# Another recorded program order for a decay-attention and feed-forward kernel, with four weight loads behind the first product

## The chip, the cores and the metric

The kernel runs on one core of one Trainium2 chip. The metric is device time in microseconds for one execution, from the start to the end of the program. The engines are named as in the profile: PE is TensorE's matmuls and PEld its weight loads, DVE is VectorE, ACT is ScalarE, POOL is GpSimd, and SP is SyncE, which here mainly issues DMAs. Each engine runs its own instructions in program order; an instruction waits by semaphores for what the others must have done first.

## The reference, cut to what matters

Four sequences (B = 4) of 768 steps go through a linear attention with eight heads of width 48 whose state decays with a complex factor. The 384 outputs of each step then go through a feed-forward layer with a rational activation.

```python
# attention: per batch b and head h, over the 768 steps t
mag = sqrt(a_re**2 + a_im**2); scale = minimum(mag, 0.999) / (mag + 1e-6)
S = (a_re + 1j * a_im) * scale * S + outer(k[t], v[t])   # the product enters the real part
y[t] = q[t] @ S.real
# feed-forward: x is y as 3072 x 384, w_in 384 x 2048, w_out 2048 x 384
h = x @ w_in
P = a0 + a1*h + a2*h**2 + a3*h**3
Q = 1 + abs(b0) * abs(h) + abs(b1) * h**2
out = (P / (Q + 1e-6)) @ w_out
```

## The kernel before, in words

**Units and pairs.** The sequence is cut into six chunks of 128 steps. A chunk of one batch is a unit; there are 24 units, in 12 pairs. Units u0 and u1 (chunk 0, batches 0 and 1) are the first pair, u2 and u3 the second. A unit goes through these functions:

- `norm`: loads the decay factors (AA), forms squares, magnitudes (three short scans, line 524, into MM) and the tangent of each step's angle (T).
- `angle` and `table`, for two units at once: sum up the angles by a scan, take off whole turns into CO and T, and take sines and cosines on ACT. A small copy (line 547, `thc`) keeps the last angle for the next chunk.
- `outer`: loads the queries and keys (QK, 384 KB) and the values (V, 320 KB); scales by the decay (`e`, line 585; line 586; `rho`, line 588; the QK product, line 589); forms two Q products (line 591), one with the cosines and one with the sines; and copies these by six DMAs of 128 KB (line 596, issued on line 345) from SBUF to SBUF into HQ, the layout that TensorE reads. There are two HQ tiles.
- `attn`: on TensorE the transposes of the keys (line 611), the scores (line 624), the values (line 642) and the states (line 662). VectorE multiplies the scores by a mask (ST, "mask product"). VectorE or ACT takes the transposes out of PSUM (kT).

**Feed-forward.** `ffn` runs once per pass. A pass has first products (line 701: x times w_in into one of three ph banks), an elementwise chain on ACT, VectorE and GpSimd, and reduce products (line 717: g times w_out). The first two passes are called with `whole`: they use fp32 weights, six instructions in a product. Later passes use split weights (wiH and wiL, wh and woL), nine in a product. The elementwise instructions are recorded by helpers, so that they have the lines of these: 351 for VectorE and GpSimd, 366 and 357 for ACT.

**Weights.** `fold` brings in w_in as 12 blocks wi (512 wide, 512 KB) and w_out as 16 blocks wo (384 wide, 384 KB). The DMA is issued on line 345; a block then takes a step on ACT (lines 431 or 439, or an equivalent on GpSimd) and two steps on VectorE (lines 447 and 449). The staging tiles are wh0 to wh2 and the four g tiles, so a load waits until a staging tile is free. `halve` later splits the weights for the passes after the second.

**Fillers.** `rouse` records matmuls without a use (line 673, into the bank po1; each shows as a pair of instructions). An order may put each on PE, or on SP, where it is no instruction at all.

**The order.** The program is first collected as a list of 2597 operations, each with its inputs (`preds`) and the engines that can run it (`ways`). The string `ORDER`, written out in the file, then fixes the place and the engine of each:

```python
code = array.array("H", zlib.decompress(base64.b85decode(ORDER)))
for step in code:
    x = (x + step) % 65536
    o = self.ops[x % 4096]
    o.eng = list(o.ways)[x // 4096]
    if not o.preds <= done:
        return None
    order.append(o)
```

The operations are emitted in this order, so it is the program order of each engine and of each DMA queue. Where an operation stands ahead of one of its inputs, `recorded` returns None and `list_schedule` searches an order by its own costs.

Of the kernel before, what the change touches and what calls it, by code (L numbers as in the profile page):

```python
# [232 lines left out]


ORDER = (
    "c-lQ!2Y8m%6@I@zJ0!U`EE#PQz)_{e5vUZEB?z(vg$gR5EKvhNnIXsq6Gen1j0izMhKwo%P-#I?P*jMvMW_`*0%5cW`EJ4pS^w#KZ>Z1z{Nww+JI;B}d){;I"
# [3 lines left out]
    "|1w8M;T41+PZqQcIsLuV!=pIXqOdSAFt2tSt=}o}E;bF&q~(c14*{&;oKQw=e#@T=o3#uU<<|Z;acprzER_oSlvjM1Yut;Gk`h=^8->OAPCmtd;+mGtm5GU-"  # L240
    "DfOGtipxa0yeJyYJYl3x2JiIBgC6Zj!WfB2$}OIYS>oxFeuZp8X)qh(xu?b`yyt8Q(B6USc5-1JVo@olgE8=QG_8#&s|rSYU8RH0Gy%t-8j)Z<FI9z`w>fgM"
    "WFu30NgHpXq$tnS!!Wca4?aMIUhR*^yAq)z%nlV^7R8xiXe}p@Dxr+|e)%J#aYXv*Q1dDlsS-bnc4WyZ`3L#7m|l2zk?+!kgfk_<t+Z#HsUZ?oGG3-jQ!hh;"
    "GKHvxVXX3yYrap|T|65F!TY>wGA)L-1)Oi8?sKTL)HCSc2%_Mb7Uc9+T$d4K_bPtdk;D0<Aimq_`h3<2tz<b8b(ERT$a<KM3Yj4b5P^C`E)z32V-fFlz%cSM"
    "8Y|UFW=npsyXWDHglXn+V^^Gy6>6A?!GmP`&IGUc5Sn3~{??DgWNEHT`~><R&bNor9GxO-ouzMz;hnS6M~-1T21$u%Wb*#K`k#J|6v-PzDc5>|B0nfu%=T##"
    "jcf9j%lT?73tpym4RxOQwBj3NFxv6Dl4EM*Wx4LRK(Q>=P4HhoONyCwHR>6EGpbaC8IIK|O)W1@l~f&yMgBy6k113sX1N+?w#oza{+}{R#vw)r<u#L~ZZi=$"
    "ubP<tI4!p$;4-fo8|69v-bOB5mPY!V^kkm?&eV!krAS64pBnHyHZTiU$qSsb9Ix=nbjiRb&J_8Us7{vua72OXVBWx)xLh+LX;e`%^W-(`<GNea5YrB;B~rKH"
    "Zl{s&hce#NsaS=<+daF>Ec{kd$mzdIJ3g6-rgA5Brajhhr$fk>R2-7eBnErrgiOW9@*v*hh>!8O6iQPZK!2i~%*glDANn=KIGkR8t9qIFl7=N@?+Cm@_1eRy"
    ")G)b%NNKBQ=&y>>AS%~yt-tVzzT7|)nZbCr!sECpE6C^<Y1=2#i&tODzZj({NWmicSUqJ@sTb?zOMEJS=gK=}J|o(LSFO;I<7RP2J&e-(%{cLc0djgQtio;M"
    "vxC@&<IMF3a8*5ImeH#h@U0$N>R}>U>j^}^y!0qF=tmhAH>xb4|Lxlx&PJXZZN8G_9B&b$CdvjX&H-LmOK-Gi1Rf@WB6C!sZ+TfO8?iu*GC?^m_hJhX@$heI"
    "*>)L(9NK)G^M}&k1@b<#;&Iy8kR!TaxLR-iCEL|3vsZqLbJAV^<bR+-%}l&)by^27gFHQ^R+<j7lm6^*`55W;-YIt9r?}1r8Nkm^WFQW6_XhlIPcChcpH!yV"  # L250
    "E{CW9XU!U7G>|&iidlM$kuO#8CIssluYuIMD^&hu-Olu8rnkf!da&P5D^o?($DkJiT70L1-0_AC<6bYxYK&2NCKi|F8zOR@PY!U`^)jA2AC$K-LAo#}j9TwU"
    "vx@vAqwzV%RY*T-)n2Z)R3>npKTAHxUn8<z$i=7BZhG5Ct;NpZ=&}X2!pUV?dzH9f;Z-B%PMOmqYCk&aC;STHkj|X2+4l=}1atJ=)UhqnM*rwvlUQ8DpTt(@"
    "8fk<gx!@G~A@pJ-I-x+?;tMsMtZ0KDXiW(#$|rIj-Q{ko;Blfi*&GaZ^a5Zs^#b2kqN(^<Yy?`;l4V5wudbSQBZB4BkW-BQ@9_vTz7_B6lBRkIt$CU{5<x|J"
    "(?4$`s9xrdsYquA1yD%*{~@)Kj5}DxAH!MI7|M)63&zpIX6Es2!Qp}Bao0_}!`Q=ko$cSGwyzSSV!67)FYbOrBJ`trn5=z(wiU>IP6^{#5kA*@SgltQ1^a42"
    "-|nV$vFJg47{S=S;^*ki%*hZu%@~OD$i5ax3vZ<Ry^4CVoLX=vaZ15mRO7CAN{{z%kl6t;;&Up4Ma0wd%nx#tJQ#uynS<B4=Fd37T6RRNg<p%c^$A+hN&bcp"
    "qyeq##XPOgxua><PppA^IHE5Zvr+ECAN6`h(Z;(6Ge&dNhmxkx`bBb>QFs<M11?E_KHn=Z;i}7wJeL(cIMyepzHkw50L!F4+V}_L8PrE6qaLBpQyGKo>cZ&r"
    "*Yu$)9%4*vUVE&+lbvSwjms_DL|wDh{Q~pIBR|h@&3$U5S;z0;y!wq>fqe!pI_+*u<kq_0$zoR`&#5%do6ox0Nk7Jjg_AWsv4dH%5D&=_b^%Gczo`_fd)=uT"
    "c3uSX<L>lIOij?!>Hhb;u41JtlfCFCRgBOIHHDVsb4~(zJqn+(lW5OuydqWVQ|?w4Y|XstjLq^Sl`w)@*_nA?A$iQt8&rl+^7UC~Ux9kWtR)UZRDmB(RU57T"
    "WQKBHv!rvhwVt`5o~Mp)RfCM}fUiiU(&nb@XWaHMH%Cx~gmt=r7@w7fUOMY@B+*)<hfo)7#=L5ognO+{>RILjy%70Goi^hoTa7o_j9D5MN;UhS39N!k*)OHj"
    "x@Hdjb7Y!Fqy{)kx5`-wi=X7%-eD$p4PZ7$-;@lU%C#5!bLin(Ji#t>F=wU8T;_(=iP!aYKMqs)YaLlK5)I`|u6CW>O#pTL^^ilqBTWuR)k-<lCX?%**CA$+"  # L260
    "yo&^ss48D%9M1{?OjUD;OEznAwb+W4Ma~YUZR}F?296reJFk*S9yPSC$D;r2Emz22nC+(}S4DCD`}%-iDO+52P1SF@8WPU<#xq*I*b^O=&iWv`>#<np#x%!s"
    ">|^gK9zm}s>I_L^^xvZ5RLCmsG@5HIVjmSkmV6|W$p2+T<-EU`$c0dc`s>#0v@Y6}^dkRB-rFL%)a!QamOqw0>`CX|(iYETQ3VyNTsU5WJrURwOGn1G2{F&q"
    ")BM*lUuNPcm2wCBuc=7q9&>R7DZyo4O3>mO$ND=A?Nzq7t8@+#Tg`J%x!C;ejFU1<zTwV4sHrB|<<D3u>RnXn=bfkNI@)w0n}4I*ntbN(0qI7bCDOte#%T|^"
    "C1i3F;(Z%_@36Ib8^-Gx^l^Dp&Q*@FaweNy%$551n`+BWY^w}rR};_=m<pbcnv<CgsT^gDasyg8gxb**OYjWQ{hFTdkh{HB{60mz68$c)T&p`ZRosfk1m<o9"
    "v*2N>iG8wGm75q9&pI2U!%P*q)JXc0jn6vHM6oX#i<Jll+0*G*#$qAsO%`><p5pQ)Gwx{Fc4k;5?ar4ACRN^%8gg-|ZswmtG?mnMr`ApCq)BHMUZOqLruXF>"
    "UQ_QN&G(!_gmEu>j_}wKc{-9jn?iovpqDSR`;7JG%3H3d7OFrPyR>O|MKAQzdB(_QM;7VkO_F5}*Fm(amU}GWx@TmGT4HV|KD5y7ltOiz#6IvmnP$%u6*5fs"
    "Fr%4`v)Mtv=QMi_US^GI%6RtIU-E?bFze%7?mw7z&t!(#U7o>TsAns6k<6wKvw0_%NVN-Y^menG*~Vv4))yi^lo>w2DgFSSNv*CX@SId8IaH!eD&6F;&eu@w"
    "?k6LX`MgMWk=c91&K`vAtd%|Kc^K}uJ(a_&7xTncj#1j`dNy~Orf2)}$nPq0xEnrV*WUvP%n8O<?CI_?7yBlx664qbA0c<<5$E^JD9LkHTC470WHzz_E@U3w"
    "@6LoLIpz*CQr2LX>c_Q?vZMZ<*fyp;hPs_>o|GASp1%=|sjuR&3&#ofohDmgBOjo>H{}O<_MLi=`r8Z_dA7Jgt0G`mjJZ{9w(<OU*;(?ae8yF(*;zeC{tXZ2"
    "dUaY<LDle_{>31Uwr032uL@3fC*2R^X=LdMPLCqU_v;+}F7GX%npTl{nd~A5^I0VsZh2te^&P`3X0hybhd35R!B#7~hUHKyH6XyX8lY5eD%;<9`VamT*jh1^"  # L270
    "&+Kk5;65A;s`w}>ko7wnmgDm=T0CzxSG67QdhR}nXE`GaCEcD1^+w-zW5c*lj<cwq%aozyZn=!m)}wWPwVKBB=R~<geXhfx?*E@E>YR|#-JR!k|2u3F%gN2o"
    "B1OLfWLuuA6n%ISvS)#=_=bI?a*?gi-NNmeU##|A<JtUvhh~ghYro4D`~OE%*PYvFC}P8ztahF8|4tx)eeV2c)w!byqvmzxz5TrNC=La?czgLPgdKPYJIiqQ"
    "|5XT9)xH?`l%3Btvfv~m;1SsdE;H?!K9;E8v};m}?0+exQs;HFV`(Mhc!5>CPRqhwrM35M{PwaZ=9Q~a;Z9@f7-l`MWqw)q=v)5@R60NE5Dh_Ht+Ux$>6D~C"
    "_pqyk5RXuYu-y93As!Y#+ojdsTHE#WJa5?OMYxfbWKfiirBgBMbp<;IYfH6=s@pZ}*EJ(yTy1;A|Bhpt{_1btu2oJg>voFZuWH9yPlua2EwkrtJKEO$m|O7)"
    "zvY)jlPbYZAWR3zo>~=VYUF=QQFeI"
)


# [830 lines left out]
```

## Time and profile before

| | |
|---|---|
| median of 3 runs | 599.2 us (598.08 to 603.07) |
| the profiled execution | 602.15 us, its span 600.5 us |
| mean granted clock of TensorE | 0.973 of full speed |
| PE busy | 558.3 us (93%) |
| PEld busy | 470.2 us (78%) |
| DVE busy | 543.7 us (91%) |
| ACT busy | 524.7 us (87%) |
| POOL busy | 284.3 us (47%) |
| instructions | 15652 |

The profile is that of one execution. The time around its span is 602.15 - 600.5 = 1.65 us. The busy times are means over the whole span; the rows below tell the stages apart.

### The profile page before, as it was taken

The numbers are of one execution on the slowest core, as the hardware profiler recorded it, in microseconds if no ns is written. First come the engines' busy times: TensorE is split into PE (matmuls) and PEld (weight loads), VectorE is DVE, ScalarE is ACT, GpSimd is POOL, SyncE is SP. The second block draws the span as 40 slices with busy tenths as digits, with TensorE's granted clock in tenths as the row PEclk, the third lists the DMA queues.
The fourth block names the chain that finished last, engine by engine and source line by source line (L and its number), as shares of the span: only waits on it lengthen the run. The fifth ranks groups of instructions, "written<-read, shape, count | busy, mean of one in ns | idle before, by whom it ended". The sixth has DMA issues, their size and how long they took to land.

```text
span 600.5 us, 15652 instructions
## 1 busy us (share of the span) xinstructions
PE 558.3 (93%) x6240; PEld 470.2 (78%) x6240; DVE 543.7 (91%) x924; ACT 524.7 (87%) x872; POOL 284.3 (47%) x253
## 2 busy tenths in 40 slices
...
GB/s 298 292 262 213 141 139 140 116 150 96 100 107 49 79 157 130 103 119 134 90 128 71 41 117 136 101 37 137 28 121 112 47 36 100 21 52 2 0 2 58
DMA packets 39185, 64.02 MB, mean 107 GB/s; under 512 B 4416, under 2 KB 25152, under 8 KB 39104
## 3 DMA queue, kind: packets, MB, share of 16 engines
...
q14 instruction: 30, 0.25, 0.1%
...
## 4 chain that ended last, share of the span: by engine, by line
PE 46%; ACT 11%; DVE 8%; issue 2%; DMA 1%; SPq 0%; DVEq 0%; ACTq 0%
PE ph L701 20%; PE po L717 19%; ACT Zf L366 4%; PE at L642 4%; PE at L624 2%; DVE Af L351 2%; ACT Af L366 2%; DVE g L351 2%; DVE ph L351 2%; PE at L662 1%; ACT L366 1%; ACT SQ L366 1%; DMA QK<-in_qk 1%; DVE Q L351 1%; PE at L611 1%
## 5 line engine op out<-in xcount | busy, mean ns | idle before, releaser
L717 PE MATMUL po<-g,wh 128*128 128x512 f32 (+1 forms) x576 | 168.2, 360 | 0.0
L701 PE MATMUL ph<-X,wiH 128*128 128x512 f32 (+1 forms) x576 | 144.2, 364 | 2.9 <-DVE Af L351 2.9
L717 PE MATMUL po<-g,wo 128*128 128x256 f32 (+1 forms) x462 | 140.3, 367 | 0.0
L717 PEld LDWEIGHTS po<-g,wh 128*128 128x128 f32 x576 | 103.1, 188 | 17.9 <-issue 1.4
L701 PEld LDWEIGHTS ph<-X,wiH 128*128 128x128 f32 x576 | 96.7, 188 | 21.8 <-issue 2.8
L717 PEld LDWEIGHTS po<-g,wo 128*128 128x128 f32 x462 | 86.9, 189 | 12.2 <-DVE ph L351 0.2
L351 POOL TENSOR_TENSOR g<-Af,Zf 128x512 fp32r<-128x512 f32 x30 | 40.0, 1333 | 100.7 <-ACT Zf L366 64.1
L366 ACT ACTIVATE Zf<-Af,co 128x512 f32<-128x512 f32 x80 | 57.8, 723 | 25.2 <-DVE ph L351 24.3
L351 DVE SCALAR_TENSOR_TENSOR ph<-Zf,co,ph 128x512 f32<-128x512 f32 x96 | 71.8, 748 | 7.1 <-ACT Zf L366 5.6
L351 DVE SCALAR_TENSOR_TENSOR g<-ph,co,Zf 128x512 fp32r<-128x512 f32 x80 | 59.6, 745 | 15.8 <-ACT Zf L366 14.1
L366 ACT ACTIVATE Af<-Af,co 128x512 f32<-128x512 f32 x96 | 69.1, 721 | 0.7
L366 ACT ACTIVATE Zf<-ph,co 128x512 f32<-128x512 f32 x96 | 65.2, 680 | 4.1 <-DVE g L351 1.5
L701 PE MATMUL ph<-X,wi 128*128 128x512 f32 (+1 forms) x264 | 67.3, 358 | 0.0
L351 DVE SCALAR_TENSOR_TENSOR Af<-Af,co,g 128x512 f32<-128x512 f32 x80 | 64.3, 804 | 2.6
L366 ACT ACTIVATE Af<-ph 128x512 f32<-128x512 f32 x96 | 56.5, 588 | 9.2 <-PE ph L701 9.1
L351 DVE SCALAR_TENSOR_TENSOR Af<-ph,co,Af 128x512 f32<-128x512 f32 x80 | 59.7, 746 | 1.2
L701 PEld LDWEIGHTS ph<-X,wi 128*128 128x128 f32 x264 | 45.7, 188 | 8.1
L366 ACT ACTIVATE Zf<-Zf 128x512 f32<-128x512 f32 x80 | 50.4, 630 | 1.9
L701 PE MATMUL ph<-wh,wi 128*128 128x256 f32 x192 | 44.8, 381 | 0.0
L351 POOL TENSOR_TENSOR RU<-MM,RU 128x384 f32<-128x384 f32 x18 | 22.7, 1259 | 39.4 <-DVE RU L351 33.4
L351 DVE TENSOR_TENSOR ST<-at,cmask 128x512 f32<-128x512 f32 x48 | 31.6, 683 | 10.1 <-ACT ph L431 4.7
L701 PEld LDWEIGHTS ph<-wh,wi 128*128 128x128 f32 x192 | 36.0, 190 | 5.1 <-PE ph L701 0.2
(204 smaller groups left out, 1103.8 us busy)
## 6 DMA issues: line engine op xcount, KB each, us to landing
HQ<-Q SPq DMA_DIRECT2D x141, 128.0 KB, 4.5
...
```

Source lines behind the costliest of these rows:

```text
L351: call = lambda e: getattr(e, kind)(*map(real, args), **{k: real(x) for k, x in kw.items()})
L366: e.activation(o(), i(), f, **kw)
L611: e.transpose(pt[:, i].bitcast(F32R), hq[:, 4 * g + i, 1, :], ident)
L624: e.matmul(pst[32 * q:32 * q + 32, i + y, s0:C], hf[:, h, 1, s0:s0 + 32], hf[:, h, 0, s0:C], start=True, stop=True)
L642: e.matmul(py[32 * y:32 * y + 32, min(j, 2), :], l, sts[h // 4][:, h % 4, :] if q is None else hf[:, h, 0, :], start=q is None and j == 0, ...
L662: e.matmul(pd[m:m + 32, h], kT[:, h, m:m + 32], V[:, n:n + D], start=True, stop=True)
L701: e.matmul(o, wt[f // 4 * NJ + j][:, f % 4 * P:f % 4 * P + P], moving(j, hl), start=n == 0, stop=n == len(prods) - 1)
L717: e.matmul(o[:, cols], wt[:, j * P:j * P + P], gg, start=(f == 0 and n == 0 and cols.start == 0), stop=(f == NFF - 1 and n == len(prods) - ...
```

## The change

The function code stays as it is. `ORDER` is another string, which decodes to the same 2597 operations:

```diff
 ORDER = (
-    "c-lQ!2Y8m%6@I@zJ0!U`EE#PQz)_{e5vUZEB?z(vg$gR5EKvhNnIXsq6Gen1j0izMhKwo%P-#I?P*jMvMW_`*0%5cW`EJ4pS^w#KZ>Z1z{Nww+JI;B}d){;I"
...
+    "c-lo+3s{y#7C!TV@Poh%79n7Qre^KBxt99ul4)6*S#DZZ-pDlX7f>ofyrp=*->-yeX(d^yC8=9!o4V<4<s~acek?0XnL%7G3g6jx=J%<G2l)BEnKS3|zVA6h"
...
 )
```

Decoded, the order of SyncE's queue up to the first feed-forward product ("|") and shortly behind it is this (AA, QK, V and HQ are the transfers of a unit, wi and wo the weight blocks):

```
before: AA u0, coef, AA u1, wo0 wi2 wi0 wo2 wo1 wi3, AA u2, QK u1, wi1, QK u0, V u1, wo3 wi4 wo5 wo4,
        V u0, wo7 wi5, HQ u0 x5, wi7, AA u3, wi8 wo6 wi6, HQ u1 x4, wo8 wo9 wo10 wi10 wo11 wi9 |
        on ACT's queue: HQ u0 x1, HQ u1 x2
after:  AA u0, coef, AA u1, wi0 wo1 wi2 wo0 wo2, AA u2, wi3, QK u1, wi1, QK u0, V u0, wi4 wo3 wo4 wo5 wi5
        wo7 wi7 wo6, HQ u0 x1, AA u3, wi6, HQ u1 x6, wi8, V u1, wo9 wo8 | wi9 wo10 wo11 wi10
        on ACT's queue: HQ u0 x5
```

So the loads of wi9, wi10, wo10 and wo11 come behind the first product. What else differs:

```
operations by engine        DVE 863 -> 855, ACT 792 -> 790, PE 420 -> 419, SP 287 -> 286, POOL 235 -> 247
fillers on PE (pairs)       31 -> 30 in all; ahead of the first product 17 -> 26, between it and the second
                            pass 12 -> 2, later 2 -> 2
outer of u0                 rho product POOL -> DVE, sine product DVE -> POOL, small copy (line 547) DVE -> POOL
                            and ahead of POOL's QK product
outer of u1                 rho product POOL -> DVE, sine product POOL -> DVE, e product DVE -> POOL;
                            QK product and cosine product stay on POOL
last product of the chain   (line 753) of later passes: 17 from DVE to POOL, 12 from POOL to DVE
VectorE's operations        ahead of u0's cosine product 30 -> 43; ahead of the first feed-forward product
                            77 -> 82; up to the one that frees the bank of the product at 121.06 us 184 -> 187
ACT's operations            ahead of the first HQ copy that reads u0's cosine product: 37 in the new order
second pass                 starts with two fillers in the new order
last five products          reduce products in both orders
```

Around 180 of the 2597 operations change their engine. `recorded` finds each input ahead of its reader in both orders.

## Rows read from the trace of the kernel before

**Rows 1.** Table of stretches: stretch (us); PE, PEld, DVE, ACT, POOL busy; PEclk, DMA, GB/s.
```profile
16.00:21.00 5.00, 4.23 (x12) 3.22 (x12) 5.00 (x8) 5.00 (x10) 3.96 (x4) 1.00 1.01 381
...
35.00:44.00 9.00, 7.89 (x156) 6.41 (x156) 8.04 (x15) 6.84 (x14) 8.79 (x9) 0.62 1.07 277
44.00:56.00 12.00, 7.66 (x109) 5.85 (x110) 6.92 (x14) 6.48 (x15) 5.04 (x7) 0.60 0.64 211
56.00:70.00 14.00, 14.00 (x107) 12.02 (x108) 13.02 (x22) 13.94 (x24) 6.44 (x9) 0.98 0.64 204
70.00:100.00 30.00, 30.00 (x274) 26.17 (x273) 29.87 (x59) 29.75 (x52) 17.81 (x17) 1.00 0.56 119
...
121.00:270.00 149.00, 146.71 (x2185) 135.65 (x2186) 144.80 (x247) 141.05 (x242) 85.36 (x71) 1.00 0.47 108
```

**Rows 2.** TensorE's timeline: start, length, instruction; in brackets the wait ahead.
```profile
35.22 0.51 PE L611 MATMUL at<-ident,HQ 128*128 128x128 f32 x4 [2.87 <-DMA HQ<-Q]
...
43.21 0.70 PE L673 MATMUL po<-Q,ident 128*128 128x256 f32 x2
...
48.34 1.23 PE L611 MATMUL at<-ident,HQ 128*128 128x128 f32 x8 [4.43 <-DMA g<-in_w_out]
...
56.70 2.75 PE L701 MATMUL ph<-wh,wi 128*128 128x256 f32 x12
...
67.97 1.99 PE L673 MATMUL po<-Q,ident 128*128 128x256 f32 x8
```

**Rows 3.** SyncE's timeline, its DMA issues into HQ (u0's, then u1's).
```profile
25.60 3.73 SPq L345 DMA_DIRECT2D HQ<-Q  x5
...
36.19 3.37 SPq L345 DMA_DIRECT2D HQ<-Q  x4
```

**Rows 4.** DMA issues from 20 to 48 us: count, KB each, median us to landing.
```profile
HQ<-Q SPq DMA_DIRECT2D x9, 128.0 KB, 6.2
...
HQ<-Q ACTq DMA_DIRECT2D x3, 128.0 KB, 7.7
```

**Rows 5.** Timelines of VectorE and TensorE at 121 us.
```profile
120.14 0.75 DVE L351 SCALAR_TENSOR_TENSOR g<-ph,co,Af 128x512 f32<-128x512 f32 x1
...
121.06 2.81 PE L701 MATMUL ph<-wh,wi 128*128 128x256 f32 x12
```

**Rows 6.** VectorE's timeline from 19 to 68 us.
```profile
19.85 2.47 DVE L351 SCALAR_TENSOR_TENSOR T<-CO,T 128x768 f32<-128x768 int32 x1
...
24.61 0.96 DVE L351 TENSOR_TENSOR Q<-QK,CO 128x768 f32<-128x768 f32 x1 [0.41 <-ACT Q L357]
...
37.48 1.01 DVE L447 SCALAR_TENSOR_TENSOR wo<-g,ph 128x384 uint32<-128x384 uint32 x2
...
51.91 0.69 DVE L351 TENSOR_TENSOR ST<-at,cmask 128x512 f32<-128x512 f32 x1 [4.70 <-ACT ph L431]
...
67.05 0.74 DVE L351 SCALAR_TENSOR_TENSOR g<-ph,co,Af 128x512 f32<-128x512 f32 x1
```

**Rows 7.** GpSimd's timeline: u0's QK product and u1's second Q product.
```profile
19.68 1.83 POOL L351 TENSOR_TENSOR QK<-QK,RU 128x768 f32<-128x768 f32 x1
...
36.11 2.24 POOL L351 TENSOR_TENSOR Q<-wh,CO 128x768 f32<-128x768 f32 x1
```

**Rows 8.** Groups by shape: count, busy us, mean ns, idle before; third: 100 to 400 us.
```profile
L351 DVE SCALAR_TENSOR_TENSOR Af<-Af,co,g 128x512 f32<-128x512 f32 x80 | 64.3, 804 | 2.6
...
L351 DVE SCALAR_TENSOR_TENSOR Af<-ph,co,Af 128x512 f32<-128x512 f32 x80 | 59.7, 746 | 1.2
...
L351 DVE SCALAR_TENSOR_TENSOR T<-CO,T 128x768 f32<-128x768 int32 x8 | 7.6, 950 | 0.2
```

**Rows 9.** ScalarE's timeline at 30 us.
```profile
30.19 0.55 ACT L439 ACTIVATE wh<-wh 128x384 int32<-128x384 uint16 x1
```

**Rows 10.** Table of stretches, columns as in rows 1: a stretch at the lower clock.
```profile
46.40:56.50 10.10, 8.16 (x110) 6.17 (x111) 5.03 (x11) 4.75 (x11) 3.51 (x6) 0.50 0.52 191
```

**Rows 11.** The chain that ended last: start, length, engine, tile, line; its end.
```profile
582.92 10.25 PE po L717 x45
```

More of the change, by code (lines that the diff above doesn't have):

```diff
@@ L235 @@
 ORDER = (
-    "c-lQ!2Y8m%6@I@zJ0!U`EE#PQz)_{e5vUZEB?z(vg$gR5EKvhNnIXsq6Gen1j0izMhKwo%P-#I?P*jMvMW_`*0%5cW`EJ4pS^w#KZ>Z1z{Nww+JI;B}d){;I"
-    "9|DiBYVi=}ens+KCJ~52D;$?7RPjkr?tzz7S>&Na0=lK~P?>nX=$bS~Ip1?IQM{zLi#<KjUyKZ?7KJl%kh4P2R|?QbT49<VV3HGe6rYfnxaK8EL}-#%9Eq_Q"
-    "$KPkUM@t;md;N^WGesVscsQlc`E4bDTDdA4^jrQW{9Rt)+!g46aKs}{M7E(VLXo7(%tdJ~ouJ@zrLV9{vgKLqmf`4)p0Y=K=0g>2Jl&h`J+f4J#g}Mt<KnCQ"
-    "+*;h19!JRy&WuKy&hR~2m78d7*o%*x_iJS&)+AbcqcD=ATObhw-Srr(N-QmU72U8~g<-RQT~6yI{wmH|ulM;OSSP>8bQskKy?swN)Ypiim$Z#*--kCO9Fue#"
@@ L240 @@
[L240 to L275, printed above, removed]
+    "c-lo+3s{y#7C!TV@Poh%79n7Qre^KBxt99ul4)6*S#DZZ-pDlX7f>ofyrp=*->-yeX(d^yC8=9!o4V<4<s~acek?0XnL%7G3g6jx=J%<G2l)BEnKS3|zVA6h"
@@ new lines @@
+    "7}ayQ`xX>USGWb0aWvgQ-?E@8W{#jb{O!^IxCx20%ca#EN4L<=Sa+OT<DF2^N(9gF?er_wRrBYt<<Y~uhr07gDuNZEMrc9nXe6(r-Z-UAYNMc_Z+J8HP`7BI"
+    "qD%rTSC?Let#}igRu~+@r?IaoWl^MRXL|7@3aIubKpprqYDhJl&Z%@7r&sa6NwUu+lt>YDFMmQ|<a2xMoklZKrv+!=(?p6<!qmtpBb1=o@?fx=^(k$*Sq87h"
+    "s7<<nzUE5#pox{|8r^g*gELeoGX!hG(w2G?N(AjvoweOzy^f-M8t3*G1uHp|EAhDuK5SDx&7V>QR$NUDnw|O(KS`hPYA&L_T%`KyQPdS)2)e|_kkK|Ok&k<^"
+    "s;cyStgjou>#6*vH@;q^jSALsFRGWqgwuY$jsDAh=$t62PeOLbA(OA@R@8{Tz^O6R0J*H^Bzl>%Xc?>u+DeD<<{UpupIZO%B#~?mu5o1A953^-_24ZU%yXOP"
@@ new lines @@
+    "mZXUB&1RIui?e<daw^hRnsK_ZI1wkzRvN&g=sv6yYCYN7MUxc2_=#dT=i^!93PIWzY3~Jlr^c53>NgcrIg4Y3AcN0q<a1^UR%Ob#vitc{nki=*-;WX=_274D"
+    "8~3NlJYL3E#L-Fr9^vy9uJ9YCO{ejtiK4=<<))$%v1H2$T2Yetv8f0~sa%sni|AQoB?1vIrCNT83uqcQpbGBK@2b(}RYtUGtU2%BDxwf~EmyJidp?f<GMYL}"
+    "KEo+=-sVX)H!ssUe>;sw<R$)Gwbm?<=k!8aE5{;33J8NA)CYJ)r71)1HdS~c!HyhWOoL!6oNj{6Tfmad6iEmCeU#23?SZl_9ON3HGQVkcX(4UL?rQ$T@7+AS"
+    "l(`*sft3>8N}JhYajePVne<Qp19(`=v*B$8$I`u6bwC}`Pa#`-{1R{=AJs^}8pC;RRUJ>{c{B;}z1A$xj|d*(LNU*er#j@vBj)q)F}c~J=bBIvVm)O9R*vJ9"
@@ new lines @@
+    "l)-I@r3W62Hg(9|E4)k$_FJfTxGkbyL@(fUK{tczg3hx2>GKks0p(E~jb&j9DTi~x(d^Xh;0iv=8&zWx=270Hu5hM)o6?bsWbF8mFUrQ|f~<ieT;(iywL&r{"
+    "nlkQ9Z_CN3;ycLFDE@_(@Ey<u#h!ZAT;qRGvFvGrd>0*;f>Mpm{w_Wtr^3Q!K85HvQXl^oAnhwz#IwK=4;nB<W|%`fk~Z>XnQb=kaI#!j!{5t`re5ByrvU%2"
+    "$e4<b$V(gPBOABTP}tt$nDIP#+KVppTR@7S-;kF+>H{4Oz4Pc}X6Ql<-kk?~8$;tFXg}~<$feYRo8j33RLi5DRLmXW;dd0R@-<FIy(V%zb;ehKvuQ7^+I`Wq"
+    "U#6QQ+=(`DId<QSGwXQ~=g?~SG9Hy(%NJ1Z{itMjc=Hikj<2RYyaSoriQM<nb(}ymsSVU&IlrNf>J@yRx^e~$v-*P5qiF~Cz^<Xxmal^qRuNyLub`4y{F(A9"
@@ new lines @@
+    "zV^d_;|O?m5*+y}jc^!W%U|+5zDSLEvl>rF^fCS(T;Hm`guTn~q5<^V_&=&unh|fLQ=XnQhz9Z&dX*2t`^}UuhnWJ@Gab>t&)f0r4aAi|ZK1DS!71Be47UV-"
+    "1pSSUfH~k6w^B9inSpfOj}WbBG2e;m{0MK4$S{*(y995eeO%7zl!DWSLYHRqx4e^%vcmq2vc1_253cY8)m_)~<G}v_ta=E)PjMSqN>CED-oamRK$W4F^r2kf"
+    "$;KR@{!|Di4yU(tjn#B|61dz9L|7KRfhU#&{owgcG!nciRa>Ej1AvTZWMBtBfqK0OJ^!=%hR>jnUDHE>r(=louQU*~y9$iI4J%LKBmp&Di&`9J+gHbd?}8qt"
+    "1lbv$Jdd{rxEuBcpuDwmkJ-U<P~UoVmwsU1M8A85N44?+p!^~F94v)`x^C^E3Y+8xI<8v+d3TzwU{EG4N7W<fI@TFPw^+}{`Vz2Xm^#Jb=DOT#9_HhGA2OQn"
```

22 lines of the change are left out of this document (added).

## Prediction

> **What bounds the kernel now.** I read the table of stretches first. [rows 1] From 56 us on TensorE is busy in every microsecond of the next two rows, and for 146.71 of the 149 us from 121 on. VectorE is busy 29.87 of the 30 us from 70 on and 144.80 of those 149. So two engines bound this kernel together: TensorE executes, VectorE feeds it. The hole lies ahead of that: between 35 and 56 us VectorE is idle for 21.00 - 8.04 - 6.92 = 6.04 us.
>
> Then TensorE's timeline. [rows 2] It waits 4.43 us for the HQ of unit u1, until 48.34, and begins the first feed-forward product at 56.70. Behind that stand filler matmuls (line 673): four pairs in 1.99 us at 67.97, so 0.50 us a pair. The label on the 4.43 us, a weight load, names the event that came last; what the transposes read is HQ, and SyncE issued the copies into it from 36.19 to 39.56. [rows 3] They took six to eight us to land. [rows 4] Last I read a product deep in the run. [rows 5] The product at 121.06 starts 0.17 us after the VectorE operation that frees its ph bank (120.14 + 0.75 = 120.89). TensorE shows no pause there, because a filler stands ahead of it. VectorE sets the pace and fillers conceal it.
>
> **The parts.** *Start of u0.* VectorE's cosine product, at 24.61 before, has 43 operations ahead of it in place of 30. [rows 6] The net 13 are four fold steps, five short scans and five 384-wide products, less a small copy. Two 384-wide steps take 1.01 us, so the second adds 0.47 (1.01 less a step's 0.54); with scans at an estimated 0.4 and two of the fold steps 512 wide at an estimated 0.6 the sum is 2 x 0.6 + 2 x 0.47 + 5 x 0.4 + 5 x 0.47 - 0.1 = 6.4 us. One saving stands against it: the step at 19.85 took 2.47 us beside GpSimd's QK product (19.68, 1.83 us), and eight later ones of its shape average 0.95. [rows 6, 7, 8] The new order has a small copy on GpSimd, ahead of that product, which reads the step's result, so the two can't meet: **-1.5 us** (bounds -1.5 and 0, if another of GpSimd's operations meets it). The product then ends at 25.57 + 6.4 - 1.5 = 30.5 us. ACT issues five of u0's six HQ copies and stands in its own queue until then; 37 of its operations are ahead of the first copy that needs this product, and before, its 37th ended at 30.19 + 0.55 = 30.74. [rows 9] So I expect no stop of ACT. The copies leave by 32.1 instead of 29.3. The transposes began 5.9 us after the last issue; I take 5.2, since V of u1 no longer stands ahead: 37.3 instead of 35.22. u0's attention ended at 43.21 + 0.70 = 43.9 and now, 2.1 later less some clock, at 45.3.
>
> *Unit u1.* Both Q products ran on GpSimd, the second until 36.11 + 2.24 = 38.35. [rows 7] Now VectorE takes one, and the rho product ahead of both. GpSimd's QK can start at 31.4, one VectorE product after u0's, and with 1.83 for it and 2.1 for the one Q it ends at 35.4, 3 us sooner. Six issues by SyncE, 0.6 each, end at 37.8 instead of 39.56. V of u1 and a block of w_in (832 KB, 0.85 MB) stood ahead of these copies and now stand behind; at the 381 GB/s of a full queue that is 2.2 us, at the 277 of the stretch itself 3.1. [rows 1] I take 2.2. Landing: 48.34 - 1.7 - 2.2 = 44.4 us, hidden by u0's work, so u1's attention begins at 45.3 instead of 48.34. It took 56.70 - 48.34 = 8.4 us, nearly all at the lower level of the clock, 1.2 GHz. [rows 2, 10] With no pause ahead of it I expect part of it at 2.4 GHz and take off 1.2 (bounds 0 and 4.2, half of it). First product: 56.7 - 3.0 - 1.2 = 52.5, **-4.2 us** on TensorE (bounds +3, if u0 is late by all of VectorE's 6.4, and -7).
>
> *The four loads.* wo10, wo11, wi9 and wi10 were issued behind u1's copies before, too, and so can't have held those up. What moves the copies is the rest of the order. The loads serve products that stand at least ten products behind the first, ten times 1.4 us. [rows 2] The queue's share falls to 0.64 and 0.56 from 56 us on. [rows 1] I cost them at nothing; that cover gone, ACT's step on a block would wait the 6 to 8 us of a landing.
>
> *Five copies on ACT.* The three that ACT issued before took 7.7 us to land, SyncE's nine 6.2. [rows 4] I count no gain. The Trainium skill, "DMA: Bandwidth & Descriptors", section "Issuing engines are not separate DMA queues", says that issuing from several engines saves only the sequencer's time, and the rows agree. Its section "Queues, rings and completion order" adds that a DMA engine takes turns between queues; by that alone the five would overtake SyncE's backlog and u0 could start some 2 us sooner.
>
> *Fillers.* Fourteen pairs stood behind the first product, now four: ten times 0.50 is **-5.0 us** of TensorE's time. [rows 2]
>
> *VectorE.* TensorE alone would end 9.2 us sooner, but not where VectorE has no time to give. Before, VectorE came to u1's mask product at 47.21 and waited 4.70. [rows 6] With 2.8 us more ahead of it (five of the early products below, and a kT copy) and the conflict gone it comes at 48.5, and the scores at 45.3 + 3.6 (51.91 - 48.34) = 48.9. So **-4.3 us** of its idle time return (bounds -6.0, the whole hole, and -1.5, if u0 is late). Against that it has more to do early: 187 operations instead of 184 up to the one that frees the bank of the product at 121.06. Seven more 384-wide products at 0.47 make 3.3; of the rest (a kT copy, a turn and an evacuation in; a split, a fold, two halvings and four small copies out) I estimate -0.5: **+2.8 us** (bounds 2.3 and 3.8, at 0.54 each). As much work stands behind that product in either order, so its lead is the lead at the end.
>
> *More on GpSimd.* It gets 12 operations more. VectorE's step with two inputs in SBUF averages 804 ns, its sister with one in PSUM 746. [rows 8] Twelve times 0.06 is **+0.7 us** (bounds 0 and 12 x 1.5 = 18, the conflict at 19.85 each time; the mean over 80 steps is the nearer row). The Trainium skill, "GPSIMD Engine Reference", section "Specifications", speaks against this change: GpSimd's SBUF interfaces are shared with VectorE, with contention for VectorE's instructions with two SBUF inputs. The row at 19.85 agrees; the mean says that it is rarely dear.
>
> The tail stays: five reduce products end the run unbroken in 10.25 us [rows 11], in the new order too.
>
> **Sum**, by VectorE: 4.3 + 1.5 - 2.8 - 0.7 = 2.3 us off the profiled span of 600.5, 598.2. With the 1.65 us around the span that is 599.85; that execution (602.15) lay 2.95 above the median of 599.2, so I predict **597 us**.
>
> **Rivals.** *TensorE alone decides.* If VectorE can give up the idle time that it has later (4.20 us from 121 to 270 alone [rows 1]), the whole 9.2 us arrive: a span of 591.3, a time of 590. For it speaks that TensorE is full; against it the 29.87 of 30 and the product at 121.06.
>
> *The clock falls, and it is slower.* Without fillers TensorE has six products of 1.4 us, one states step of 0.8 and two pairs, 10.2 us of work, from 52.5 to 62.7. The fourth pair needs the bank that VectorE freed at 67.05 + 0.74 = 67.8 [rows 6]; now that comes 5.8 sooner and 2.7 later, at 64.7. A pause of 4.43 us before was followed by 10.1 us at half clock [rows 2, 10], 5 us of work lost, and VectorE stands as well. One such fall costs 2 + 5 and eats most of the 9.2: no change. A second one, at the start of the second pass where two fillers remain, makes it slower: 598.2 + 10 = 608, a time of 607. Against it: the pause at 62.7 is half as long as the one that cost the clock.
>
> *The order isn't taken.* The planner searches anew if an operation stands ahead of one that it needs. Decoded, all 2597 stand once and behind their inputs: no chance.
>
> **How the numbers follow.** 0.52 for the forecast and what lies near it (one fall of the clock; none of the idle time back, which gives 602.5 - 2.95 + 1.65 = 601), 0.25 for TensorE alone, 0.23 for the slower case. One per cent, 6 us, is about what a measurement of this kernel can tell; only the first rival is faster by more, 0.25, and only the second slower, 0.23. The forecast's own range is 593 to 602, from the bounds of the idle time and of the early work. For eight in ten I go from 590 to 606, up to the first rival and most of the way to the second.
>
> **What would show it.** u1's transposes at about 45 us without a wait of 4, the first product at 52 to 53, VectorE 1 to 2.5 us idle between 35 and 56, the step of 19.85 at 1 us. If the product of 121.06 starts at about 119, VectorE paces and the sum is right; at 113 it doesn't. A stretch at half clock behind 56 us would be the slower rival. It is wrong if u0's transposes start after 39, if ACT stops for over 2 us at its copies, or if the order makes TensorE pause deep in the run, which no count of operations shows.

## The result and the profile after

The new order takes 608.17 us (median of 4 runs, 607.38 to 609.90) against 599.29 us (598.08 to 603.07): a ratio of 1.0138, 95% interval 1.0099 to 1.0176. It is slower by 1.4%, outside the range of 590 to 606 us that was given eight chances in ten. The profiled execution took 608.0 us, its span 606.3. VectorE is busy for 553.3 us in it; before it was 543.7, with eight operations more. In the changed kernel each line number behind the order string is smaller by one; in the kernels of the experiments it differs by a few.

The table of stretches of the new order, columns as in rows 1:

```profile
35.00:44.00 9.00, 4.95 (x17) 3.81 (x16) 6.05 (x12) 6.29 (x12) 4.61 (x7) 0.71 1.04 195
44.00:56.00 12.00, 11.09 (x249) 9.39 (x252) 8.94 (x18) 8.59 (x16) 6.67 (x10) 0.79 0.93 268
56.00:70.00 14.00, 12.44 (x124) 10.03 (x113) 13.54 (x23) 13.50 (x24) 10.69 (x12) 1.00 0.56 192
70.00:100.00 30.00, 28.27 (x192) 24.00 (x191) 29.65 (x54) 29.82 (x54) 17.72 (x20) 1.00 0.63 151
121.00:270.00 149.00, 146.88 (x2212) 136.19 (x2211) 145.68 (x248) 142.29 (x239) 89.78 (x73) 1.00 0.48 110
```

VectorE's idle time between 35 and 56 us is 21.00 - 6.05 - 8.94 = 6.01 us, where 6.04 stood before [rows 1]: it moved from the second row to the first, and nothing of it came back. TensorE has pauses from 56 to 100 us (1.56 and 1.73 us in the two rows) where it had none, and its clock stays at 1.00 there.

TensorE's timeline, first of u0's transposes, then of u1's, the first product, and two later pauses:

```profile
43.38 0.72 PE L610 MATMUL at<-ident,HQ 128*128 128x128 f32 x4 [4.05 <-DMA HQ<-Q]
...
51.94 0.99 PE L610 MATMUL at<-ident,HQ 128*128 128x128 f32 x8
...
57.30 3.07 PE L700 MATMUL ph<-wh,wi 128*128 128x256 f32 x13
...
68.77 1.53 PE L700 MATMUL ph<-wh,wi 128*128 128x256 f32 x6 [1.56 <-DVE g L350]
...
73.90 4.15 PE L700 MATMUL ph<-wh,wi 128*128 128x256 f32 x18 [1.02 <-DVE g L350]
```

u0 begins 8.2 us later than in rows 2, u1 no longer waits, and the first product comes 0.6 us later (57.30 against 56.70). That is one execution of each order. Where other kernels have the same order up to there, the first product came at 50.37 to 54.20 us in four with before's order (the three of "more work" below and before_short) and at 54.78 to 57.75 in four with after's (mid_after and the three that cut after's products). So the profiled execution of before was a late one, and the new order lies more than 0.6 us behind here, some 2 us by the middle ones.

Why u0 is late stands in ScalarE's timeline, in two loads that SyncE issued earlier, and in the DMA issues from 20 to 48 us (count, KB each, median us to landing):

```profile
30.70 3.08 ACTq L344 DMA_DIRECT2D HQ<-Q  x2
33.83 0.52 ACT L430 ACTIVATE ph<-g 128x384 f32<-128x384 f32 x1 [3.55 <-DVE wi L446]
35.46 0.56 ACTq L344 DMA_DIRECT2D HQ<-Q  x1
```

```profile
25.37 0.33 SPq L344 DMA_DIRECT2D g<-in_w_out  x1
25.79 0.38 SPq L344 DMA_DIRECT2D g<-in_w_in  x1
```

```profile
HQ<-Q SPq DMA_DIRECT2D x7, 128.0 KB, 8.0
HQ<-Q ACTq DMA_DIRECT2D x5, 128.0 KB, 8.4
```

u0's cosine product ended at 30.67 us, but the last copy of it was issued from 35.46 to 36.02. The line of 3.08 us holds two issues of 0.55 us each, at 30.70 and 33.23, and a wait between them. The trace names what the later ones waited for. The program's transfers use eight semaphores in turn, and each waits until the transfer eight issues ahead of it has landed. For the copy at 33.23 that was the w_out block issued at 25.37, which landed at 33.21; for the one at 35.46 it was the w_in block issued at 25.79, which landed at 35.44. In before's trace no issue stands right behind such a landing. The fold step between them (line 430, at 33.83) had its bank from 33.44 on and stood behind the copy. The last copy landed at 43.02, and the transposes began at 43.38.

The start explains little of the total, though. VectorE's operation that frees the bank of the product of 121.06 us [rows 5] ends here at 121.45 + 0.75 = 122.20, so the new order lies 1.3 us behind at that point, and the whole span 5.8. Matched by number, the first products of the two traces stay within about 2 us of each other up to 364 us, but for stretches in which the two orders have some products at other places; then the new order falls some 3 us back within five. GpSimd's timeline there, VectorE's, and TensorE's:

```profile
361.35 1.84 POOL L350 TENSOR_TENSOR Q<-QK,T 128x768 f32<-128x768 f32 x1
364.50 1.01 POOL L350 TENSOR_TENSOR SQ<-SQ 128x384 f32<-128x384 f32 x1 [1.31 <-ACT SQ L365]
...
366.28 2.24 POOL L350 TENSOR_TENSOR Q<-QK,CO 128x768 f32<-128x768 f32 x1
```

```profile
361.42 2.05 DVE L350 TENSOR_TENSOR_SCAN MM<-MM,ncar,SQ 128x128 f32<-128x128 f32 x1
...
364.70 1.24 DVE L350 SCALAR_TENSOR_TENSOR RU<-Z,RU 128x384 f32<-128x384 f32 x1
365.86 0.99 DVE L350 SCALAR_TENSOR_TENSOR Af<-Af,co,g 128x512 f32<-128x512 f32 x1
366.89 0.75 DVE L350 SCALAR_TENSOR_TENSOR Af<-ph,co,Af 128x512 f32<-128x512 f32 x1
367.67 1.39 DVE L350 TENSOR_TENSOR g<-Af,Zf 128x512 fp32r<-128x512 f32 x1
```

```profile
369.12 0.73 PE L716 MATMUL po<-g,wh 128*128 128x512 f32 x2 [2.00 <-DVE g L350]
```

The short scan takes about 0.48 us elsewhere. Here it starts 0.07 us after a GpSimd product, stands until that ends at 363.19, and ends at 363.47. The RU step (0.55 elsewhere), an Af step and g are stretched in the same way. The step at 366.89 lies beside GpSimd's product as well, but one of its inputs is in PSUM; it takes its usual 0.75. TensorE then waits 2.00 us for g.

Over the whole run the groups by form (count, busy us, mean ns, idle before) show the same; after:

```profile
L350 DVE SCALAR_TENSOR_TENSOR Af<-Af,co,g 128x512 f32<-128x512 f32 x80 | 69.9, 873 | 2.8
L350 DVE SCALAR_TENSOR_TENSOR Af<-ph,co,Af 128x512 f32<-128x512 f32 x80 | 59.7, 746 | 1.6
L350 DVE TENSOR_TENSOR_SCAN MM<-MM,ncar,SQ 128x128 f32<-128x128 f32 x69 | 33.9, 498 | 1.2 <-ACT SQ L356 1.2
L350 DVE SCALAR_TENSOR_TENSOR T<-SQ,T 128x384 f32<-128x384 f32 x23 | 14.2, 619 | 0.1
L350 DVE SCALAR_TENSOR_TENSOR RU<-Z,RU 128x384 f32<-128x384 f32 x23 | 13.9, 604 | 0.1
L350 DVE SCALAR_TENSOR_TENSOR SQ<-AA,SQ 128x384 f32<-128x384 f32 x23 | 13.8, 599 | 0.1
```

and the last four of these in the kernel before (its first two are in rows 8):

```profile
L351 DVE TENSOR_TENSOR_SCAN MM<-MM,ncar,SQ 128x128 f32<-128x128 f32 x69 | 31.3, 477 | 0.0
L351 DVE SCALAR_TENSOR_TENSOR SQ<-AA,SQ 128x384 f32<-128x384 f32 x23 | 13.0, 564 | 0.2
L351 DVE SCALAR_TENSOR_TENSOR RU<-Z,RU 128x384 f32<-128x384 f32 x23 | 12.8, 555 | 0.0
L351 DVE SCALAR_TENSOR_TENSOR T<-SQ,T 128x384 f32<-128x384 f32 x23 | 12.5, 545 | 0.1
```

With equal counts, five groups with all inputs in SBUF grew by 5.6 + 2.6 + 1.7 + 1.1 + 0.8 = 11.8 us. They are the ones that grew most; some others shrank, and all groups of equal counts together grew by 10.4 us. The group with an input in PSUM took 59.7 us both times, and it is the control that the trace brings along. An estimate over all of VectorE's operations says the same. Take from each the usual length of its form, the median over the traces of all these kernels: the operations without an input in PSUM that lie beside one of GpSimd's took 14.2 us more than usual in before and 23.4 in after, and those with one in PSUM that lie beside GpSimd 0.6 us in both.

### The profile page after: what moved, and what is told of

It is laid out like the page before. It is cut to its first block, busy times and chain, and to the rows that moved or that the text cites. A ratio compares the mean times of both kernels' runs of the same rounds, so it can differ in the third digit from the quotient of the medians.

```text
span 606.3 us, 15669 instructions
## 1 busy us (share of the span) xinstructions
PE 560.2 (92%) x6238; PEld 470.1 (78%) x6238; DVE 553.3 (91%) x916; ACT 522.8 (86%) x866; POOL 294.8 (49%) x265
## 4 chain that ended last, share of the span: by engine, by line
PE 52%; DVE 18%; ACT 6%; issue 4%; DVEq 0%; ACTq 0%
PE po L716 23%; PE ph L700 20%; DVE Af L350 6%; DVE g L350 4%; PE at L641 4%; ACT Zf L365 3%; DVE ph L350 3%; PE at L623 3%; PE at L661 1%; PE at L610 1%; DVE ST L350 1%; ACT Af L365 1%; DVE RU L350 1%; DVE QK L350 1%; DVE MM L350 0%
## 5 line engine op out<-in xcount | busy, mean ns | idle before, releaser
L350 POOL TENSOR_TENSOR g<-Af,Zf 128x512 fp32r<-128x512 f32 x35 | 47.1, 1345 | 110.6 <-DVE Af L350 75.5
L350 DVE SCALAR_TENSOR_TENSOR Af<-Af,co,g 128x512 f32<-128x512 f32 x80 | 69.9, 873 | 2.8
L350 DVE SCALAR_TENSOR_TENSOR Af<-ph,co,Af 128x512 f32<-128x512 f32 x80 | 59.7, 746 | 1.6
L350 POOL TENSOR_TENSOR Q<-QK,CO 128x768 f32<-128x768 f32 x14 | 28.5, 2038 | 28.6 <-ACT CO L564 9.9
L350 POOL TENSOR_TENSOR Z<-MM,Z 128x384 f32<-128x384 f32 x20 | 22.3, 1115 | 32.7 <-ACT Z L365 32.7
```

The lines of the kernel that those rows point to most:

```text
L350: call = lambda e: getattr(e, kind)(*map(real, args), **{k: real(x) for k, x in kw.items()})
```

## The experiments

Four theories are tried in pairs. First *S*, the loss lies in the start, against *L*, it lies in the later order. Then *G*, it is VectorE's time beside GpSimd's operations, against *P*, it is the places in the order and their waits. All kernels decode to the same 2597 operations unless the text says otherwise, and each ratio is to runs of the kernel before on the same chip.

**The two halves exchanged.** The order was cut at the first feed-forward product, and the rest taken from the other order.

```diff
# start_before
-ORDER: after
+ORDER: operations 0 to 243 of before, then what is left in the order and on the engines of after
# start_after
-ORDER: after
+ORDER: operations 0 to 251 of after, then what is left in the order and on the engines of before
```

> The order of before up to the first feed-forward product, and behind it all that is left in the order of after, with after's engines. Theory S (the loss lies in the start, where u0's transposes stand at 43.38 us instead of 35.22): the loss is gone, 599 to 600 us. Theory L (the loss lies in the later order: VectorE beside GpSimd, as in the pause of TensorE at 366 us): it stays, 605 to 609 us.

> The mirror: after's order up to the first feed-forward product, then before's order and engines. Theory S: 606 to 609 us. Theory L: 598 to 602 us. If both this and its mirror lie half way, the two halves share the loss.

Measured: 608.36 us, ratio 1.0137 (1.0111 to 1.0163), with before's start; 602.84 us, 1.0031 (1.0000 to 1.0062), with after's. So the later order carries the loss, and theory S falls: the start with u0's 8 us costs some 0.3%, by the interval no more than 0.6% (602.84 is a little above what L gave). VectorE's busy time, from the first part of the two pages, goes the same way:

```profile
PE 559.2 (92%) x6238; PEld 469.1 (77%) x6238; DVE 552.9 (91%) x913; ACT 524.6 (86%) x870; POOL 294.5 (48%) x264
```

```profile
PE 557.4 (93%) x6238; PEld 468.6 (78%) x6238; DVE 545.1 (90%) x926; ACT 523.6 (87%) x869; POOL 282.4 (47%) x254
```

**A cut at 340 us.**

```diff
-ORDER: after
+ORDER: operations 0 to 1649 of after, then what is left as in before
```

> After's order up to operation 1650 of 2597, the place that after reaches at 340 us, then before's order. In the two traces TensorE's work stands level up to 364 us (within 2 us) and after is 4.2 us behind from 384 us on. Theory L: no more than 2 us above before, 599 to 602 us. Theory S, or a loss spread evenly over the run: 603 to 609 us.

Measured: 604.61 us, 1.0077 (1.0044 to 1.0110), in the range given for a loss spread over the run and above L's. The pause at 366 us is not all: by the middles of the intervals, each some 0.3% wide to either side, of the 1.38% some 0.31 (1.9 us) come with the start, 0.46 (2.8 us) more up to 340 us, and 0.61 (3.7 us) behind that. The single pair of profiled executions, level until 364 us, had shown too little of the middle part.

**The four loads alone.**

```diff
-ORDER: before
+ORDER: before, with the loads of wi9, wo10, wo11, wi10 right behind the first product
```

> Before's order with nothing but the loads of wo11, wi9, wo10 and wi10 moved behind the first product (one step of ScalarE on wo10's block follows its load). Both theories, and the prediction, cost these loads at nothing: 598 to 601 us. If the loads alone are the matter: 604 or more.

Measured: 602.44 us, 1.0016 (0.9980 to 1.0052): no difference that can be told. The part of the change that its name speaks of does nothing.

**Engines and places exchanged in bulk.**

```diff
# after_engines_before: after's places, before's engines behind the first product; after_g_before: for line 753 alone
# before_engines_after: before's places, after's engines; before_g_after: for line 753 alone
-        o.eng = list(o.ways)[x // 4096]    # as recorded with the place
+        o.eng = the engine that the other order records for the same operation
```

> After's order, but behind the first product each operation that both orders let run on VectorE, ScalarE or GpSimd takes the engine that it had before (55 from GpSimd to VectorE, 42 back, and 35 others). Theory G (the loss is VectorE's time beside GpSimd, made by which operations GpSimd gets): VectorE's busy time falls from 553 to some 546 us and the time to 598 to 602 us. Theory P (the loss is made by the places in the order, whichever engine works): 605 to 609 us.

> The mirror: before's order and start, with after's engines behind the first product. Theory G: 604 to 609 us, VectorE busy for about 550 us or more. Theory P: 598 to 602 us. If both this and its mirror are slow, a choice of engines and an order belong together, and neither theory holds alone.

> After with the engines of before for the last product of the chain alone (line 753 of before: 17 from GpSimd back to VectorE, 12 from VectorE back to GpSimd). Theory G, if these carry it: 600 to 604 us; if the products of the attention part on GpSimd carry it: 606 to 609 us, as after.

> Before with after's engines for the last product of the chain alone. The prediction costed the five more of these on GpSimd at some tenths of a us: 598 to 601 us. If the 17 new places meet VectorE's two-input operations: 602 to 607 us.

Measured, in this order: 679.14 us, 1.1283 (1.1202 to 1.1364); 650.97, 1.0835 (1.0760 to 1.0911); 632.21, 1.0533 (1.0455 to 1.0612); 621.58, 1.0331 (1.0259 to 1.0404). Neither theory said that; the second expectation had named the case that both are slow. An engine seems to belong to its place: an operation that GpSimd may run at leisure was recorded early, and on VectorE it makes everything behind it wait. VectorE's group of the cosine products shows an instance, 7.4 us of idle time ahead of it in the first of the four and 0.6 in before (columns as above); the rest of that loss wasn't taken apart:

```profile
L348 DVE TENSOR_TENSOR Q<-QK,CO 128x768 f32<-128x768 f32 x8 | 9.6, 1206 | 7.4 <-POOL QK L348 4.7 <-ACT CO L562 2.6
```

```profile
L351 DVE TENSOR_TENSOR Q<-QK,CO 128x768 f32<-128x768 f32 x8 | 9.3, 1162 | 0.6 <-ACT Q L357 0.4
```

These four don't tell G from P, since each makes new waits; they show that in both orders engines and places are fitted to each other.

**More work on GpSimd.** Rows 96 to 127 of the tile St are unused, and smask is constant.

```diff
             o.emit(E)
+            at_ += 1
+            if 1400 <= at_ < 2360 and at_ % 60 == 0:
+                nc.gpsimd.tensor_tensor(St[96:P, 0, 0:384], half, half, ALU.mult)      # before_dose
+                # before_dose_small: six tensor_copy of three columns in its place
```

> Before, with 16 products of 384 columns more on GpSimd, one behind every 60th operation from the 1400th to the 2340th. They read a constant and write into rows that nothing reads, so no engine waits for their results; by the Z row each takes about 1.0 us. Theory G: where one meets a two-input operation of VectorE it holds it up, and VectorE's busy time and the total rise by 4 to 12 us, 603 to 612. If beside-work on GpSimd costs VectorE nothing that counts: 598 to 602 us.

> The control: at the same 16 places six GpSimd copies of three columns each, some 0.18 us apiece by the row of the small copies, so about the same 1.1 us of GpSimd's time with hardly any data. If what counts is the data that GpSimd moves while VectorE wants its own, 598 to 602 us; if it is GpSimd's time (its own later products come later, or any instruction of its own holds VectorE up), as with the wide products, 603 to 612 us.

Measured: 604.10 us, 1.0060 (1.0033 to 1.0086), for the wide products, and 602.57, 1.0034 (1.0005 to 1.0064), for the small copies. GpSimd's groups of the two (the copies took 0.25 us apiece, so the control spent the longer time):

```profile
L1058 POOL TENSOR_TENSOR St<-smask 32x384 f32<-32x384 f32 x16 | 15.8, 989 | 1.3
```

```profile
L1059 POOL COPY St<-smask 32x3 f32<-32x3 f32 x96 | 19.4, 251 | 1.0
```

Work that no one waits for costs the kernel some 3.6 us, as G wants it, though at the low end. The control isn't clean: it cost 2 us itself, and the intervals overlap. It also moves GpSimd's later products, which then meet others of VectorE's.

**More work on VectorE.**

```diff
-                nc.gpsimd.tensor_tensor(St[96:P, 0, 0:384], half, half, ALU.mult)
+                nc.vector.tensor_tensor(St[96:P, 0, 0:384], half, half, ALU.mult)
```

> Before with 16 products of 32 x 384 more on VectorE instead of GpSimd, at the same 16 places as the wide GpSimd products; nothing reads them. At 0.54 us each (the row of the 384-wide products) that is 8.6 us of VectorE's time. If VectorE sets the end in the later part, as the prediction has it: 605 to 610 us. If TensorE does and VectorE has time to give: 599 to 602 us.

Measured: 611.16 us, 1.0193 (1.0154 to 1.0232), for this VectorE group:

```profile
L1058 DVE TENSOR_TENSOR St<-smask 32x384 f32<-32x384 f32 x16 | 13.9, 870 | 0.4
```

13.9 us of VectorE's time cost 11.6 us of the total (600.26 x 0.0193). VectorE sets the pace in the later part. (The total is a little above the range given, which had 0.54 us for each product; they took 0.87.)

**Fewer fillers.**

```diff
-ORDER: before
+ORDER: before, the 12 filler pairs between the first product and the second pass on SP (no instruction)
```

> Before without the 12 filler pairs that stand between the first product and the second pass. TensorE alone would end 12 x 0.50 = 6.0 us sooner: 593 to 595 us. If VectorE sets the pace there and the fillers only cover its time: 598 to 602 us, with pauses of TensorE between 60 and 100 us. If the clock falls in these pauses: 603 to 608 us.

Measured: 603.69 us, 1.0033 (0.9999 to 1.0067), with two pauses of TensorE where fillers had stood:

```profile
65.75 2.83 PE L698 MATMUL ph<-wh,wi 128*128 128x256 f32 x12 [2.91 <-DVE g L348]
...
75.03 2.93 PE L714 MATMUL po<-g,wo 128*128 128x256 f32 x6 [2.85 <-DVE g L348]
```

The total lies in the range that was given for a fall of the clock, and the granted clock was 0.89 from 70 to 100 us. Of the 6 us that were taken from TensorE none came back. In the first passes the pauses stand where the fillers had been and end with VectorE's g, so the fillers conceal VectorE's time there. The total alone doesn't show it: VectorE was also busy for 548.9 us in this execution, 5.2 more than in before, and the clock took its share.

**u0's last copies on SyncE.**

```diff
-two of u0's cosine copies into HQ: ACT
+two of u0's cosine copies into HQ: SP
```

> After with the last two of u0's cosine copies into HQ issued by SyncE instead of ScalarE, at the same place in the order. If ScalarE's own queue held them (the last left at 35.46 us, behind a step that waited for VectorE until 33.83), u0's transposes begin at 38 to 40 us instead of 43.38. The total: by theory L as after, 605 to 609 us; if u0's lateness cost the time, 599 to 603 us.

Measured: 610.09 us, 1.0164 (1.0135 to 1.0192). u0 began at 41.62 instead of 43.38, not at 38 to 40. The two copies left by 32.05 instead of 36.02, but SyncE stood for them with four weight loads behind, and u0's sixth copy, behind these loads, now left last:

```profile
30.55 1.50 SPq L342 DMA_DIRECT2D HQ<-Q  x2
...
34.71 0.55 SPq L342 DMA_DIRECT2D HQ<-Q  x1
```

The delay went from one queue to the other. With u0 1.8 us sooner the total isn't lower, one more sign that the start isn't what counts.

**GpSimd's products cut short.** Nothing is moved: the same instructions, places and waits.

```diff
-        mul(2 * W, lambda: QK.t, lambda: QK.t, lambda: RU.t, (QK, r0, r1), (QK,), eng=EN["qru"])
+        mul(2 * W, lambda: QK.t, lambda: QK.t, lambda: RU.t, (QK, r0, r1), (QK,), eng=EN["qru"], short=c > 0)
...
-                ways[e] = (..., call)
+                ways[e] = (..., few if e == "POOL" and short else call)   # few: the same call on 16 columns of each 128
```

> Before, with the QK and Z products that GpSimd does in chunks 1 to 5 cut to 16 columns of each stretch of 128 (the rest of the result stays unscaled: part of the computation is left out). Order, engines and waits stay. Beside these products VectorE lost 1.3 us in the profiled execution of before (0.39, 0.48 and 0.46), so theory G gives 597 to 600 us. Theory P (places and waits alone) gives the same.

> After with the same cut of GpSimd's QK and Z products. Six of the costly meetings of after are with these (0.78 and 0.62 at 170 and 323 us, 0.81, 1.28, 1.22 and 0.73 at 181, 350, 380 and 418 us), 5.4 us in all. Theory G: the distance to the cut version of before shrinks from some 8 us to 2 to 5 us. Theory P: it stays at 7 to 9 us.

Measured: 600.35 us, 0.9998 (0.9973 to 1.0024), and 602.02 us, 1.0026 (0.9998 to 1.0054). The distance between the two orders falls from 1.38% to 0.28%, or 1.7 us. P alone, which has it stay, falls. What is left is no more than the start, which this cut doesn't touch, had cost (0.31%).

VectorE's busy time is a weaker witness. In the profiled executions it is 548.6 and 550.2 us, a distance of 1.6 in place of 9.6, but only 3.1 us of this come from after (553.3 to 550.2). Before's rose by 4.9 (543.7 to 548.6), against what G gave, and its total didn't change. So a microsecond that VectorE loses beside GpSimd isn't one of the total everywhere. After's span fell by 6.0 us (606.3 to 600.3); the 3.1 are half of that, and in the other half VectorE waited less.

**Six of them, against six others.** The cut also lets GpSimd's results come earlier, and this pair takes that out.

```diff
# after_short_hit
+ QK: short=(c, bb) in {(2, 0), (4, 1), (4, 2)}      Z: short=(c, bb) in {(2, 0), (4, 0), (5, 0)}
# after_short_miss
+ QK: short=(c, bb) in {(2, 1), (4, 0), (4, 3)}      Z: short=(c, bb) in {(2, 1), (4, 1), (5, 1)}
```

> After with only six of GpSimd's products cut to 16 columns of each 128: the three QK and three Z products (at 171, 181, 323, 350, 380 and 418 us) beside which VectorE's operations were stretched by 0.62 to 1.28 us, 5.4 us in all (part of the computation is left out). If these meetings carry a part of the loss: 602 to 606 us, 2 to 5 us below after. If the cut helped because GpSimd's own results came earlier: as in the control.

> The control: after with three other QK and three other Z products of the same units' neighbours cut in the same way (at 195, 199, 332, 337, 402 and 450 us), beside which VectorE showed no stretch over 0.25 us. GpSimd gains the same time. If the meetings carry the loss: as after, 606 to 609 us. If GpSimd's earlier results do: as with the six others, 602 to 606 us.

Measured: 605.16 us, 1.0074 (1.0044 to 1.0104), where the six had met VectorE's operations, and 608.96 us, 1.0148 (1.0109 to 1.0187), where they had not. The intervals are just apart, and the control is as slow as after. In after's trace no other engine waits for any of the twelve products, so that earlier results are no likely cause. One of the meetings, at 350 us, in VectorE's timeline, first with the six cut, then in the control:

```profile
351.57 0.75 DVE L350 SCALAR_TENSOR_TENSOR Af<-Af,co,g 128x512 f32<-128x512 f32 x1
```

```profile
350.19 2.13 DVE L350 SCALAR_TENSOR_TENSOR Af<-Af,co,g 128x512 f32<-128x512 f32 x1
```

In the control GpSimd's QK product ran from 349.94 for 1.83 us beside it. In the profiled execution with the six cut four of the six meetings are gone; the one at 170 us stays, since VectorE's operation had begun beside another of GpSimd's products, the one at 323 is shorter, and others came up (0.8 us each at 196 and 396). VectorE's busy time is 553.1 us there and 553.7 in the control, and that execution is one of the slower of its kernel at 606.8 us. So the size of 3.8 us rests on the medians, not on that trace.

## Why the prediction was wrong

In the profiled spans the forecast was 598.2 us and 606.3 was measured, 8.1 more. Two terms make this up: the 4.3 us of VectorE's idle time that were to return and didn't, and the later order beside GpSimd, costed at 0.7 us, which cost 4.5 behind the product of 121.06 us in this pair. The forecast then took off 2.95 us because before's execution lay that far above its median; after's lay 0.17 us below its own.

**What bounds the kernel: right.** VectorE paces in the later part (13.9 us more on it cost 11.6), and fillers conceal it in the first passes (without 12 pairs TensorE waited for VectorE's g, and nothing was gained).

**The start of u0: right up to the product, wrong behind it.** The step that had met GpSimd's QK product took 0.95 instead of 2.47 us, the -1.5; the cosine product ended at 30.67 where 30.5 was worked out. "So I expect no stop of ACT" failed. ScalarE stood idle for 3.55 us, and the copies had left by 36.02 instead of 32.1, because the last two waited for the landings of weight loads that SyncE had issued eight to ten microseconds ahead. From the last issue to the transposes it took 7.4 us in place of 5.2: they began at 43.38, not 37.3. Counting ScalarE's operations ahead of the copies told when the queue would reach them, not what each of these waits for.

**u1 and the idle time: the first term that failed.** u1 needn't wait any more, as said. But with u0 6 us later than worked out it began at 51.94 instead of 45.3, and the first product came at 57.30 instead of 52.5. The -4.3 us of returned idle time measured 0.03. Before's 6.04 us was itself a high value: in the four other executions with its order VectorE was idle for 1.2 to 4.7 us between 35 and 56, in the four others with after's for 3.6 to 6.0.

**Early work on VectorE: its agreement is luck.** At the product of 121.06 us the terms -1.5 and +2.8, with nothing for the idle time, give +1.3, and this pair measured +1.3. But the operation that frees that bank ended at 114.67 to 120.39 us in the four others with before's order, and at 120.05 to 123.56 in the four others with after's (in before_short and after_short a few products are cut by then). The middle ones of five, 118.50 and 122.20, lie 3.7 us apart, so the terms aren't shown at this size. Of a lag at this point not all reaches the end: the start alone (start_after) cost some 1.9 us.

**The loads, the copies' queue and the fillers: right.** The loads alone gave 1.0016, no change that the interval tells, and the fillers' 5 us of TensorE never reached the end. The five copies on ACT gained nothing: they took 8.4 us to land, SyncE's seven 8.0. The Trainium skill, "DMA: Bandwidth & Descriptors", section "Queues, rings and completion order", has a DMA engine take turns between queues, by which they would have overtaken SyncE's backlog. In the new order they didn't: the copy that ScalarE issued at 28.00 landed at 36.35, behind the block that SyncE had issued at 25.79 (35.44) and ahead of the one issued at 29.61 (38.87). With three of them left on ScalarE's queue (after_hq_sp) these took 3.2 us and SyncE's nine 8.5, but that doesn't bear on it: SyncE stood still from 23.62 to 30.55 us there, and the first two found no other transfer under way.

**"More on GpSimd", +0.7 us: the second term that failed, and the larger in the totals.** It counted twelve operations times the difference of two means. But a meeting isn't priced by how many operations GpSimd has; it depends on which of VectorE's operations starts while one of GpSimd's is under way, and for how long that one still runs. In the new order five groups of VectorE's operations grew by 11.8 us. The upper bound of 18 us had held this; the value was taken from the mean of an order whose places make such meetings cheaper. By the ratios the later order costs 1.38 - 0.31 = 1.07%, 6.4 us, in place of 0.7; with GpSimd's QK and Z products cut, 0.28% (1.7 us) are left of the whole 1.38. The Trainium skill, "GPSIMD Engine Reference", section "Specifications", names the mechanism, GpSimd's SBUF interfaces shared with VectorE, with contention for VectorE's instructions with two SBUF inputs. The traces agree: 804 to 873 ns with both inputs in SBUF, 746 in both with one in PSUM.

**The slower rival** named the clock. The clock stayed at 1.00 from 56 to 350 us, and fell only behind the pause at 366 us (0.93 from 350 to 375 us); slower it was, but not by that mechanism.

What stays open: why before lost no time in its cut version though VectorE was busy for 4.9 us more, that is, which meetings cost the total something and which don't (the Q and g products weren't cut, as a tile must be written whole); and why the meetings are more here. They hang on moments that differ by tenths of a microsecond.
